# Attention in pairs of units: another order of one core's products, with norm weights and value pads made on chip

## The chip, the core and the metric

The kernel runs on one core of a Trainium2 chip. The core has five engines, each with an instruction queue of its own: TensorE (PE, with its weight loads listed as PEld), VectorE (DVE), ScalarE (ACT), GpSimd (POOL) and SyncE (SP, which here issues nearly all DMAs). They meet through semaphores. The metric is the device time of one execution in microseconds.

## What is computed

Three stages: attention with a bias that a small network computes from positions, a gated layer behind an RMS norm, and a layer with a squared ReLU.

```python
def _attn_ref(q, k, v, w1, b1, w2):          # q, k, v: 2 x 8 x 576 x 64
    scores = scale * np.matmul(q, k.transpose(0, 1, 3, 2))
    x = (psi_rel / psi_i)[..., None]         # log1p of distance / log1p of row
    h = np.maximum(x @ w1 + b1, 0.0)         # 32 hidden values per pair of positions
    bias = h @ w2                            # 8 heads
    scores = scores + bias.transpose(2, 0, 1)[None, :, :, :]
    scores = scores - np.max(scores, axis=-1, keepdims=True)
    attn = np.exp(scores)
    attn = attn / (np.sum(attn, axis=-1, keepdims=True) + 1e-09)
    return np.matmul(attn, v)
def _moe_ref(x, w_gate, w_val, w_out, rms_g):    # 1152 x 512, 1536 wide
    xn = x / np.sqrt(np.mean(x * x, axis=-1, keepdims=True) + 1e-06) * rms_g
    g = xn @ w_gate
    return (g * (1.0 / (1.0 + np.exp(-g))) * (xn @ w_val)) @ w_out
def _moe2_ref(x, w_in, w_out, s, b):             # 2048 wide
    r = np.maximum(x @ w_in, 0.0)
    return (s * (r * r) + b) @ w_out
```

## The kernel before

**Units.** Attention works on nine token tiles of 128 rows (eight of one batch each, the ninth with 64 rows of both). A tile is four units, each a pair of heads, so there are 36 units, `u` from 0 to 35. What is done for a unit:

- *scores* (`scores_mm`, L235): 64x64 products of q and k for both heads into the two buffers of `psA`, two PSUM banks each.
- *soft* (L248), once for each head `e`: one DVE operation adds the bias row and takes the row minimum of the negated sum. *expo* (L260): ACT's exponential with the row sum.
- *turn* (`turn_mm`, `turn_out`, L266 to L282): nine 128x128 transposes into `psB`, four for each head (`e0`, `e1`) and one for the rest of both (the tail). ACT evacuates e0 and the tail; DVE evacuates e1, but for every fourth unit from 6 to 29, where ACT does.
- *values* (`values_mm`, L284): products with v on 128x32 tiles into the one bank of `psO`.

**Bias rows.** 36 groups `g` of 16 rows. `hide(g)` (L176) computes the hidden values `hq`, four operations of 304 to 576 columns; from group 12 on POOL does one of them and DVE three. `bias_mm` (L189) is one visit of PE on 128x32 tiles, into one bank of `psB` or two where there are more than 512 columns; `bias_out` (L205) is two or three ACT operations. Groups 0 to 7 go to the bias buffer at once, the others are stored to DRAM (`rows`) and come back skewed by `bias_in` (L215). `bias` has two buffers, one for each chunk of two tiles.

**Finishing a tile.** `finish_a`: ACT copies `psO` out. `finish_t`: four PE transposes. `finish_b`: DVE divides by the row sums. `finish_s`: DVE sums squares, POOL raises to the power -1/2 (`rstd`). `finish_n` (L341): DVE scales by `rstd` and the norm weights `g_bc`. `finish_c`: four transposes, ACT's cast (L350) and DVE's subtraction (L351) give the high and the low part of `xs`, the operand of the next stage.

**Order.** The schedule is manual: each engine executes in the order in which the program writes its instructions. The loop at L473 runs step `s` once per unit: bias products of one group (`groups(s)`), scores of unit s+1, transposes of s, values of s-1, with one finishing function per step and `hide(s+13)`. `psB` has three banks in turn, `pr` (the exponentials) and `pt` (the transposed ones) two buffers each. `PT_DVE`, `SUMS`, `TAIL` and `BITS` (L452 to L455) tell at which steps operations of the next stage are issued: weights are fetched, clamped, put together from the bits of 64-bit numbers and split, and POOL makes sums of `xs`. After the loop the products of the next stage begin (`prod`, L624).

**Loads.** k and v tiles are loaded one per step on SP; a v tile is 128 x 10 x 64 with two half slots of zeros that come from DRAM with it. `g_bc` is loaded with a DMA that repeats one row on 128 partitions.

## Time and profile before

| | us |
|---|---|
| median of three runs (lowest, highest) | 599.57 (599.15, 600.49) |
| the profiled execution | 599.94 |
| its span, first to last instruction | 598.1 |
| PE busy in the span | 591.7 |
| DVE busy | 437.0 |
| ACT busy | 337.8 |
| POOL busy | 233.5 |

Busy time says who works, not who is waited for: the end of a matmul is modelled, so a PE that is 99% busy may still be at less than its peak. What a stage is bound by is read from its own window, and there from the steps between the starts of PE's groups: an interval that repeats to a hundredth of a us and has no releaser beside it is PE's own; one that varies, with a wait in brackets, is somebody else's. An idle engine costs nothing unless it is waited for.

### The profile page before, as it was taken

The page shows a single profiled execution, that of the slowest core. Times are in us where ns is not written, and L with a number is a line of the kernel's source. Part 1 is how long each engine was busy: PE and PEld are TensorE (multiplying, and loading weights), DVE is VectorE, ACT ScalarE, POOL GpSimd, SP SyncE. Part 2 cuts the span into 40 slices and gives each one's busy share as a digit, 9 for nine tenths or more (in the row PEclk, how much of TensorE's full clock was granted, in tenths as well). Part 3 has the DMA queues.
Part 4 walks back from the last instruction along what each step waited for, and adds up shares of the span by engine and source line. Part 5 has one row for each costly group of instructions (what it writes and reads, how often), then busy time and mean ns, then how long its engine had stood idle before and what let it go on. Part 6 is the DMA issues. An engine that isn't in the chain of part 4 may idle for free.

```text
span 598.1 us, 13403 instructions
## 1 busy us (share of the span) xinstructions
PE 591.7 (99%) x5370; PEld 529.1 (88%) x5370; DVE 437.0 (73%) x791; ACT 337.8 (56%) x689; POOL 233.5 (39%) x209
## 2 busy tenths in 40 slices
PE   9999999999999999999999999999999999999997
PEld 5466666667779999999999999999999999999996
DVE  7977888976876887788788944568778445888741
ACT  7887887887765555555657432255554235555210
POOL 0424334622446655655644432322224233222430
PEclk9999999999999999999999999999999999999999
DMA  6899445465112232133222323212222322222421
GB/s 213 265 321 258 151 148 146 149 205 155 37 39 71 71 110 103 71 102 110 72 75 102 103 74 105 105 38 73 86 83 101 118 71 70 71 72 70 162 86 53
DMA packets 25885, 67.52 MB, mean 113 GB/s; under 512 B 3136, under 2 KB 4704, under 8 KB 25824
## 3 DMA queue, kind: packets, MB, share of 16 engines
q1 hardware_dynamic: 25776, 66.66, 34.6%
q8 instruction: 42, 0.69, 0.5%
q14 instruction: 19, 0.16, 0.1%
q10 hardware_dynamic: 48, 0.02, 0.0%
HBM read 53.47 MB, written 10.83 MB: 108 GB/s over the span
## 4 chain that ended last, share of the span: by engine, by line
PE 74%; DVE 15%; ACT 5%; issue 4%; POOL 2%; DMA 1%; DVEq 0%; ACTq 0%; SPq 0%; POOLq 0%
PE c L624 11%; PE b L624 7%; PE po L302 7%; PE a L244 6%; PE b L272 6%; PE c L601 5%; DVE f L857 5%; PE c L599 5%; PE c L600 5%; DVE hv L853 4%; PE b L189 3%; PE b L601 3%; PE b L600 3%; PE b L599 3%; ACT f L856 3%
## 5 line engine op out<-in xcount | busy, mean ns | idle before, releaser
L408 POOL TENSOR_TENSOR wlo<-wa,whi 128x512 fp32r<-128x512 f32 (+1 forms) x71 | 92.7, 1308 | 89.5 <-ACT whi L405 89.5
L382 POOL TENSOR_SCALAR wa<-wa 128x512 f32<-128x512 f32 x68 | 45.7, 672 | 118.0 <-ACT wa L381 111.2
L256 DVE CUSTOM_DVE_ANT_0 sn<-a,bias 128x576 f32<-128x576 f32 x72 | 51.7, 754 | 19.3 <-PE a L244 11.8
L381 ACT ACTIVATE wa<-wraw 128x512 f32<-128x512 f32 x68 | 45.7, 673 | 27.1 <-DMA wraw<-in_wo 23.7
L263 ACT ACTIVATE pr<-sn,nm 128x576 f32<-128x576 f32 x72 | 56.3, 782 | 1.5 <-DVE nm L256 1.5
L176 POOL TENSOR_SCALAR hq<-tab,c_sb,thr 128x384 f32<-128x384 f32 (+17 forms) x24 | 45.7, 1911 | 28.8 <-DMA bias<-br 20.5
L857 DVE SCALAR_TENSOR_TENSOR f<-hv,b_sb,f 128x384 fp32r<-128x384 f32 x48 | 39.6, 824 | 21.9 <-ACT f L856 21.9
L856 ACT ACTIVATE f<-hv,b_sb 128x384 fp32r<-128x384 f32 x48 | 29.6, 617 | 45.4 <-DVE hv L853 45.3
L405 ACT CAST whi<-wa 128x512 fp32r<-128x512 f32 x68 | 41.9, 617 | 19.8 <-DVE wa L393 19.5
L601 PE MATMUL c<-f,wlo 128*128 128x384 f32 (+1 forms) x150 | 49.9, 333 | 0.7 <-POOL wlo L408 0.7
L600 PE MATMUL c<-f,whi 128*128 128x384 f32 (+1 forms) x150 | 49.7, 331 | 0.0
L599 PE MATMUL c<-f,whi 128*128 128x384 f32 (+1 forms) x150 | 49.7, 331 | 0.0
L390 DVE TENSOR_SCALAR wa<-wa 128x512 int32<-128x512 int32 x46 | 28.8, 625 | 25.4 <-POOL wa L382 25.4
L302 PE MATMUL po<-pt,vs 128*32 128x128 f32 (+1 forms) x1600 | 46.8, 264 | 0.0
L624 PE MATMUL c<-xs,whi 128*128 128x384 f32 x184 | 46.8, 335 | 0.0
L244 PE MATMUL a<-ks,q 64*64 64x352 f32 (+1 forms) x576 | 44.5, 415 | 0.2 <-ACT br L205 0.2
L281 ACT COPY pt<-b 128x512 f32<-128x512 f32 (+1 forms) x78 | 33.2, 435 | 20.4 <-PE b L272 20.1
L302 PEld LDWEIGHTS po<-pt,vs 128*32 128x32 f32 x1600 | 37.7, 110 | 5.8 <-issue 5.7
L244 PEld LDWEIGHTS a<-ks,q 64*64 64x64 f32 x576 | 18.9, 132 | 26.8 <-issue 6.3
L272 PEld LDWEIGHTS b<-ident,pr 128*128 128x128 f32 x288 | 30.8, 140 | 12.2 <-issue 9.6
L176 DVE TENSOR_SCALAR hq<-tab,c_sb,thr 128x448 f32<-128x448 f32 (+17 forms) x87 | 40.3, 524 | 0.0
L272 PE MATMUL b<-ident,pr 128*128 128x128 f32 x288 | 39.6, 280 | 0.3 <-ACT pr L263 0.3
(188 smaller groups left out, 1624.7 us busy)
## 6 DMA issues: line engine op xcount, KB each, us to landing
wraw<-in_wo SPq DMA_DIRECT2D x28, 512.0 KB, 3.5
bias<-rows SPq DMA_DIRECT2D x32, 288.0 KB, 4.3
rows<-br SPq DMA_DIRECT2D x28, 295.5 KB, 3.1
wraw<-in_win SPq DMA_DIRECT2D x16, 512.0 KB, 3.5
wraw<-in_wg SPq DMA_DIRECT2D x12, 512.0 KB, 3.6
wraw<-in_wv SPq DMA_DIRECT2D x12, 512.0 KB, 3.7
vs<-in_v SPq DMA_DIRECT2D x8, 320.0 KB, 6.4
ks<-in_k SPq DMA_DIRECT2D x8, 288.0 KB, 5.8
```

What stands on the lines that cost most here:

```text
L176: eng.tensor_scalar(hq, src, w1_sb, thr[:, n:n + 1], op0=ALU.mult, op1=ALU.max)
L244: nc.tensor.matmul(ps[e][qc, f], qt[u // 4][ed, hp, qc], ks[b[i % len(b)] * NP + hp][ed, f], start=True, stop=True, tile_position=(e * D, ...
L256: nc.vector.tensor_tensor_reduce(out=sn, in0=ps, in1=bias[chunk(u)][:, h, :], scale=-1.0 / SCALE, scalar=3.0e38, op0=ALU.add, op1=ALU.min, ...
L263: nc.scalar.activation(prs[u][:, e * S:(e + 1) * S], sn, AF.Exp, bias=nm, scale=-1.0, accum_out=sums[u // 4][:, h:h + 1])
L272: nc.tensor.transpose(pT[:, c * P:(c + 1) * P], pr[:, o:o + P], ident)
L302: nc.tensor.matmul(dst, w, a, start=c == 0, stop=c == NQC - 1, tile_position=(0, o))
L408: nc.gpsimd.tensor_tensor(out=lo[:, c:c + step], in0=w[:, c:c + step].bitcast(F32), in1=hi[:, c:c + step].bitcast(F32), op=ALU.subtract)
L599: nc.tensor.matmul(ps, hi[:, ws], ah, start=first, stop=False)
L600: nc.tensor.matmul(ps, hi[:, ws], al, start=False, stop=False)
L601: nc.tensor.matmul(ps, lo[:, ws], ah, start=False, stop=last)
L624: nc.tensor.matmul(ps, w[i][:, (c0 + c) * P:(c0 + c + 1) * P], a[h][c], start=first and c == 0 and i == 0 and h == 0, stop=c == 1 and i == ...
L857: nc.vector.scalar_tensor_tensor(out=hl[:, cols(j)], in0=g2, scalar=b_sb, in1=hh[:, cols(j)].bitcast(F32), op0=ALU.add, op1=ALU.subtract)
```

## The change

The loop takes two units at a time: a step of an even `s` issues scores of s+1 with soft and expo, values of s-2 and s-1, the bias products and `hide` of two groups, scores of s+2 with soft, and then all eighteen transposes of s and s+1 (`turns`), with the exponentials of s+2 put in between. The tails of two units share a bank and one copy. `finish_t` and `finish_c` are issued within the transposes, the rest of finishing around them. `pr` gets a third buffer. The loads of k and v are listed by step (`LOADS`), and all rows that have been stored are loaded at the start of a step. The tables of the next stage's operations get even steps.

The norm weights come as one row with 128 ones behind it (`g_row`); a product of the ones with the row puts it on all partitions, and ACT copies it to `g_bc` before the first pair. The v tiles come without zeros, in two halves of 64 partitions whose slots are shifted against each other, and DVE writes the zeros.

```diff
-    pr_p = ring(att, "pr", 2, "right")
+    pr_p = ring(att, "pr", 3, "right")
     pt_p = ring(att, "pt", 2, "right")
+    tail_p = ring(att, "ptl", 1, "right")
...
+    g_row = tab_p.tile([1, DM + P], F32, name="g_row")
...
+    nc.sync.dma_start(out=g_row, in_=rms_g)
...
-    vs = [None] * (B * NP)
+    vs = [ac.tile([P, 10, D], F32, name=f"vs{n}") for n in range(B * NP)]
+    for t in vs:
+        for h in range(2):
+            nc.vector.memset(t[D - h * D:P - h * D, 9 * h], 0.0)
...
     def load_v(n):
-        t = ac.tile([P, 10, D], F32, name=f"vs{n}")
-        nc.sync.dma_start(out=t, in_=v[:, n])
-        vs[n] = t
+        for h in range(2):
+            ps = slice(h * D, h * D + D)
+            nc.sync.dma_start(out=vs[n][ps, h:h + 9], in_=v[ps, n])
...
-    load_v(0)
-    nc.sync.dma_start(out=g_bc, in_=rms_g.partition_broadcast(P))
...
-    def turn_mm(u, e):
-        pr = prs[u]
-        pT = psB.tile([P, 512], F32, name="b")
-        if e < 2:
+    def turns(s, mid):
+        us = [u for u in (s, s + 1) if u < NU]
+
+        def turn(u, e):
+            pT = psB.tile([P, 512], F32, name="b")
             for c in range(4):
                 o = e * S + e * D + c * P
-                nc.tensor.transpose(pT[:, c * P:(c + 1) * P], pr[:, o:o + P], ident)
-        else:
-            nc.tensor.transpose(pT[:, :P], pr[:, 512:640], ident)
-        return pT
-
-    def turn_out(u, e, pT):
-        w = 512 if e < 2 else P
-        t = pt_p.tile([P, w], F32, name=f"pt{e}")
-        on_act = e not in PT_DVE or 6 <= u < 30 and u % 4 == 2
-        (nc.scalar.copy if on_act else nc.vector.tensor_copy)(t, pT[:, :w])
-        pts[u, e] = t
+                nc.tensor.transpose(pT[:, c * P:(c + 1) * P], prs[u][:, o:o + P], ident)
+            t = pt_p.tile([P, 512], F32, name=f"pt{e}")
+            on_act = e not in PT_DVE or 6 <= u < 30 and u % 4 == 2
+            (nc.scalar.copy if on_act else nc.vector.tensor_copy)(t, pT)
+            pts[u, e] = t
+
+        order = [(u, e) for e in range(2) for u in us]
+        for i, (u, e) in enumerate(order):
+            if i == 3:
+                mid["e0"]()
+                mid.pop("fin", bool)()
+            turn(u, e)
+        mid.pop("fin", bool)()
+        if us:
+            pT = psB.tile([P, 512], F32, name="b")
+            for i, u in enumerate(us):
+                nc.tensor.transpose(pT[:, i * P:(i + 1) * P], prs[u][:, 512:640], ident)
+            t = tail_p.tile([P, 2 * P], F32, name="pt2")
+            nc.scalar.copy(t, pT[:, :2 * P])
+            for i, u in enumerate(us):
+                pts[u, 2] = t[:, i * P:(i + 1) * P]
+        mid["e1"]()
...
-                    w, a = (vt[:, 4 * e + c, d:d + 32], pm[e][:, c * P + c0:c * P + c0 + cols]) if c < 4 else \
-                        (vt[:, 8 + e, d:d + 32], tl[:, c0:c0 + cols])
+                    w, a = (vt[:, 1 + 4 * e + c, d:d + 32], pm[e][:, c * P + c0:c * P + c0 + cols]) if c < 4 else \
+                        (vt[:, 9 * e, d:d + 32], tl[:, c0:c0 + cols])
...
-    SUMS = [(26, s_full, (0, 0, 0)), (27, s_full, (3, 0, 2)), (28, s_full, (1, 1, 0)), (29, s_full, (2, 1, 2)),
-            (31, s_comb, (2, 1, 2, ALU.add)), (36, s_comb, (1, 0, 1, ALU.subtract))]
+    SUMS = [(26, s_full, (0, 0, 0)), (26, s_full, (3, 0, 2)), (28, s_full, (1, 1, 0)), (30, s_full, (2, 1, 2)),
+            (30, s_comb, (2, 1, 2, ALU.add)), (34, s_comb, (1, 0, 1, ALU.subtract))]
...
-    TAIL = [(22, w_fetch, 0), (22, w_fetch, 1), (27, w_clamp, 0), (28, w_clamp, 1), (31, w_split, 0), (31, w_fetch, 2),
-            (33, w_clamp, 2), (34, w_split, 1), (34, w_fetch, 3)]
-    BITS = {30: 0, 33: 1}
+    TAIL = [(22, w_fetch, 0), (22, w_fetch, 1), (26, w_clamp, 0), (30, w_clamp, 1), (32, w_split, 0), (32, w_fetch, 2),
+            (34, w_clamp, 2), (34, w_split, 1), (34, w_fetch, 3)]
+    BITS = {28: 0, 32: 1}
...
+    pg = psO.tile([P, 512], F32, name="po", tag="po")
+    nc.tensor.matmul(pg, g_row[:, DM:], g_row[:, :DM], start=True, stop=True)
...
-    for s in range(-2, NU + 1):
-        r = s % 4
-        if s >= 5 and r == 1:
-            finish_a(s // 4 - 1)
...
+    def steps(s):
+        return [x for x in (s, s + 1) if s > -1] or [s]
+
+    LOADS = {0: ((load_k, 3), (load_v, 0), (load_k, 4), (load_v, 1)),
+             2: ((load_k, 5), (load_v, 2), (load_v, 3), (load_k, 6)),
+             4: ((load_k, 7), (load_v, 4), (load_v, 5)), 6: ((load_v, 6), (load_v, 7))}
+
+    for s in [-2, -1] + list(range(0, NU + 2, 2)):
+        both = steps(s)
+        new = [u for u in ((s + 1,) if s < 0 else (s + 1, s + 2)) if 0 <= u < NU]
+        for x in both:
+            if x >= 0 and x % 4 == 0:
+                load_q(x // 4 + 1)
+            if x == -1:
+                load_k(2)
+        for fn, n in LOADS.get(s, ()):
+            fn(n)
+        if s == 6:
+            xs = [act_p.tile([P, NKC, NT], F32R, name=f"xs{i}", tag=f"x{i}") for i in range(2)]
+        landed = list(rows)
+        if s >= 0:
+            for g in landed:
+                bias_in(g)
...
+        if s == -1:
+            for g in landed:
+                bias_in(g)
+            ps = scores_mm(0)
+            groups(s)
+            keep_clock(3)
+            soft(0, 0, ps[0])
+            expo(0, 0)
+            soft(0, 1, ps[1])
+            expo(0, 1)
+            nc.scalar.copy(g_bc, pg)
+            hide(12)
+            continue
+        if s + 1 < NU:
+            ps = scores_mm(s + 1)
+            for e in range(2):
+                soft(s + 1, e, ps[e])
+                expo(s + 1, e)
         if s in BITS:
...
+        if s % 4 == 0:
+            next(part, None)
+        if s >= 6 and s % 4 == 2:
+            finish_n(s // 4 - 1)
+        for u in (s - 2, s - 1):
+            if u >= 0:
+                values_mm(u)
+        if s >= 4 and s % 4 == 0 and s <= NU - 4:
+            finish_a(s // 4 - 1)
+        for x in both:
+            groups(x)
+        for x in both:
+            hide(x + 13)
+        if s + 2 < NU:
+            ps = scores_mm(s + 2)
+            for e in range(2):
+                soft(s + 2, e, ps[e])
+        mid = {"e0": lambda: s + 2 < NU and expo(s + 2, 0), "e1": lambda: s + 2 < NU and expo(s + 2, 1)}
+        if s >= 4 and s % 4 == 0 and s <= NU - 4:
+            mid["fin"] = lambda: finish_t(s // 4 - 1)
+        if s >= 6 and s % 4 == 2:
+            mid["fin"] = lambda: finish_c(s // 4 - 1)
+        if s % 8 == 4:
+            for g in list(rows)[:1]:
+                bias_in(g)
+        turns(s, mid)
+        if s >= 4 and s % 4 == 0 and s <= NU - 4:
+            finish_b(s // 4 - 1)
+            finish_s(s // 4 - 1)
         next(part, None)
...
+        for x in both:
+            for at, fn, n in TAIL:
+                if at == x:
+                    fn(n)
+            for at, fn, arg in SUMS:
+                if at == x:
+                    fn(*arg) if fn is s_full else fn(arg)
...
-    va = np.zeros((P, B * NP, 10, D), np.float32)
-    va[:, :, 0:4] = vv[:, 0, :512].reshape(B * NP, 4, P, D).transpose(2, 0, 1, 3)
...
                                keep, w2blk, minv, mrow], axis=1),
```

## Rows read from the trace of the kernel before

**Rows 1.** Windows: length, busy us (count) by engine, PEclk, DMA, GB/s.

```profile
98.16:116.97 18.81, 18.81 (x312) 11.88 (x308) 16.64 (x39) 14.94 (x36) 9.88 (x5) 1.00 0.49 144
116.97:135.09 18.12, 18.12 (x329) 12.25 (x317) 13.69 (x33) 14.84 (x38) 3.48 (x2) 1.00 0.61 183
139.16:154.31 15.15, 15.15 (x270) 10.88 (x269) 10.78 (x26) 12.08 (x31) 7.48 (x7) 1.00 0.36 95
```

**Rows 2.** Timeline of PE without bias rows: start us, us, line, op, tiles.

```profile
142.66 1.20 PE L244 MATMUL a<-ks,q 64*64 64x352 f32 x16
143.79 1.09 PE L272 MATMUL b<-ident,pr 128*128 128x128 f32 x8
144.72 0.27 PE L274 MATMUL b<-ident,pr 128*128 128x128 f32 x1
144.92 1.30 PE L302 MATMUL po<-pt,vs 128*32 128x128 f32 x40
146.15 1.20 PE L244 MATMUL a<-ks,q 64*64 64x352 f32 x16
...
149.64 0.66 PE L347 MATMUL b<-ident,x 128*128 128x128 f32 x4
150.23 1.20 PE L244 MATMUL a<-ks,q 64*64 64x352 f32 x16
```

**Rows 3.** Timeline of PE while bias rows are computed.

```profile
83.28 0.66 PE L315 MATMUL b<-ident,oT 128*128 128x128 f32 x4
83.86 0.91 PE L189 MATMUL b<-hq,c_sb 128*32 128x416 f32 x8
...
91.18 1.30 PE L302 MATMUL po<-pt,vs 128*32 128x128 f32 x40
92.30 0.93 PE L189 MATMUL b<-hq,c_sb 128*32 128x448 f32 x8
93.16 1.20 PE L244 MATMUL a<-ks,q 64*64 64x352 f32 x16
```

**Rows 4.** Timeline of PE's weight loads (PEld), one unit.

```profile
90.05 0.86 PEld L272 LDWEIGHTS b<-ident,pr 128*128 128x128 f32 x8 [0.33 <-issue]
...
92.19 0.24 PEld L189 LDWEIGHTS b<-hq,c_sb 128*32 128x32 f32 x8
```

**Rows 5.** Timeline of DVE; in brackets the idle time before, and its releaser.

```profile
106.50 1.46 DVE L176 TENSOR_SCALAR hq<-tab,c_sb,thr 128x512 f32<-128x512 f32 x3
...
110.81 0.74 DVE L341 SCALAR_TENSOR_TENSOR x<-x,rstd,g_bc 128x512 f32<-128x512 f32 x1
111.47 2.15 DVE L176 TENSOR_SCALAR hq<-tab,c_sb,thr 128x528 f32<-128x528 f32 x3
...
135.81 0.69 DVE L351 TENSOR_TENSOR xs<-b,xs 128x512 fp32r<-128x512 f32 x1 [1.41 <-ACT xs L350]
...
144.00 0.76 DVE L256 CUSTOM_DVE_ANT_0 sn<-a,bias 128x576 f32<-128x576 f32 x1 [1.44 <-PE a L244]
```

**Rows 6.** Timeline of POOL in the bias stage.

```profile
107.45 9.09 POOL L176 TENSOR_SCALAR hq<-tab,c_sb,thr 128x512 f32<-128x512 f32 x4
```

**Rows 7.** Timeline of ACT and PE at the start of attention.

```profile
25.46 1.10 ACT L205 ACTIVATE br<-b,cb,c_sb 128x400 f32<-128x400 f32 x2
...
29.00 1.09 PE L272 MATMUL b<-ident,pr 128*128 128x128 f32 x8
...
29.70 0.59 ACT L281 COPY pt<-b 128x512 f32<-128x512 f32 x1
```

**Rows 8.** Timeline of the first us: DVE's first work, PE's first bias products.

```profile
2.82 0.30 DVE L155 TENSOR_SCALAR thr<-c_sb 128x144 f32<-128x144 f32 x1 [2.82 <-DMA c_sb<-in_cst]
...
6.02 11.80 PE L189 MATMUL a<-hq,c_sb 128*32 128x512 f32 x128
```

**Rows 9.** Timeline of PE: scores of unit 35, first product behind.

```profile
169.47 1.20 PE L244 MATMUL a<-ks,q 64*64 64x352 f32 x16
...
177.55 0.60 PE L624 MATMUL b<-xs,whi 128*128 128x384 f32 x2
```

More of the change, by code (lines that the diff above doesn't have):

```diff
@@ L410, in w_split @@
             wst[n] = hi, lo
-    NU = 4 * NTT
     NG = S // 16
@@ L508, in tile_kernel @@
-        if 0 <= s + 1 < NU:
-            expo(s + 1, 1)
-        next(part, None)
-        if s >= 6 and r == 2:
-            finish_s(s // 4 - 1)
-        if s >= 7 and r == 3:
-            finish_n(s // 4 - 1)
-        if s >= -1:
-            hide(s + 13)
+        if s % 4 == 0:
[7 more added lines that the diff above has]
+            finish_a(s // 4 - 1)
@@ L519, in tile_kernel @@
             nc.sync.dma_start(out=b_sb, in_=b_p)
-        if 0 <= s - 1 < NU:
-            values_mm(s - 1)
-        if s >= 5 and r == 1:
-            finish_t(s // 4 - 1)
-        if s == 6:
-            xs = [act_p.tile([P, NKC, NT], F32R, name=f"xs{i}", tag=f"x{i}") for i in range(2)]
-        if s >= 8 and r == 0:
-            finish_c(s // 4 - 2)
         if s == 26:
@@ L956, in _layout @@
         "cst2": np.concatenate([np.tile(f["w2"], (1, 16)), f["b1"].reshape(HID, 1)], axis=1),
-        "rms_g": f["moe_rms_g"],
+        "rms_g": np.concatenate([f["moe_rms_g"], np.ones(P, np.float32)])[None],
         "wg": tile_up(f["moe_w_gate"], 12), "wv": tile_up(f["moe_w_val"], 12),
```

46 lines of the change are left out of this document (10 added, 36 removed).

## The prediction

> **What bounds the kernel now.** I read the table of windows first. In the three windows of the attention stage PE is busy for the whole window at a granted clock of 1.00, while DVE has 16.64 of 18.81 us while bias rows are still computed, 13.69 of 18.12 where they end and 10.78 of 15.15 behind them; ACT lies at 14.94, 14.84 and 12.08, POOL lower [rows 1]. Since the end of a matmul is modelled, I checked a full PE against its timeline: every unit repeats at the same step and no line shows a wait. Without bias rows a unit is scores 1.13 us (142.66 to 143.79), nine transposes 1.13 (to 144.92), values 1.23 (to 146.15): 3.49 us [rows 2]. With bias rows it is longer by one group of bias products: 0.86 where 448 columns are computed [rows 3]. So PE's instruction stream sets the time of this stage, and an order that costs PE less is worth its full saving, as long as nobody becomes late. DVE is nearest to that: 88% in the first window [rows 1].
>
> The stage behind attention is products on PE from 177.55 on [rows 9]; I take an earlier end of attention to move all of it. The profiled execution took 599.94 us (span 598.1 and 1.84 around it), the median of the runs is 599.57. I sum against 599.94 and subtract 0.37 at the end.
>
> **The change, part by part.**
>
> *PE's order.* The PE instructions of a unit stay; their order goes from (bias, scores, transposes, values) per unit to (scores, values x2, bias x2, scores, transposes x18) per pair. What that is worth are the places where PE changes from one kind of tile to another. Values followed by bias products, the same 128x32 tile, take 1.12 (91.18 to 92.30) [rows 3]; followed by scores 1.23 [rows 2]: a change there costs 0.11. Eight transposes take 0.93 (143.79 to 144.72), so 0.116 each, and the ninth with its change 0.20: 0.084. Four transposes before scores take 0.59 [rows 2] against 4 x 0.116 = 0.465 inside a run: 0.125. Per pair I get
> - one change bias to scores, or values to scores, less: 0.11;
> - transposes 2 x 1.13 = 2.26 become 18 x 0.116 + 0.125 = 2.22: 0.04 less;
> - one visit of scores is now left towards values and not towards transposes. No row shows that. It costs at most the same 1.13 and at least 0.11 less, as if there were no change. What is exposed first is a weight load: eight of 128 columns take 0.86, eight of 32 columns 0.24 [rows 4], 0.107 and 0.03 each. I take the difference, 0.08 less.
>
> Together 0.23 per pair (0.15 to 0.26); 16 pairs stand between scores of unit 4 and scores of unit 35: **-3.7 us** (-2.4 to -4.2).
>
> *Finishing.* The two times four transposes of a token tile move into the run of transposes. While bias rows are computed one costs 0.58 (83.28 to 83.86) [rows 3] and the values ahead 0.11 more, 0.69; without bias rows 0.59 [rows 2]. Inside a run it is 0.465. Nine of the 15 in the loop stand in the bias stage, six behind it: 9 x 0.225 + 6 x 0.125 = **-2.8 us**.
>
> *New waits.* This is the other side. A run of transposes now fills five banks of the three of psB in a row, so each waits for the evacuation three before it. An evacuation by ACT starts 0.70 after its first transpose (29.00 to 29.70) and takes 0.59 [rows 7], the third bank behind it begins 3 x 0.465 = 1.40 later: just in time on ACT. In the eight pairs with finish_a, e1 of the first unit is copied by DVE behind two soft, some 0.1 late: 0.8 us in all. In the pairs with finish_c the DVE subtraction L351 waits for ACT's cast, which now stands behind an exponential. DVE stood still 1.41 us for that cast before [rows 5]; now e1's copy and the next soft are queued behind it, and scores wait for soft to free psA.
>
> How late it gets depends on the hidden rows. Both units' hq now stand in one block between soft of the first and soft of the second unit. Pair 18, from the start of its first scores: e1's copy, finish_b and finish_s of the pair before, three operations of 512 columns like finish_n (0.66, 110.81 to 111.47) and 0.4 of small ones, hold DVE to 2.2; two soft, about 0.7 each, to 3.6; finish_n to 4.2; six hq, which take 1.46 per three alone but 2.15 while POOL works too [rows 5], and POOL has its own four for 9.09 us [rows 6]: 4.0, to 8.2. The second scores start at 4.95 (1.05, 2 x 1.12, some 1.65 for two bias groups), and soft could start 1.34 behind (142.66 to 144.00) [rows 2, 5], at 6.3. It is through with psA at 9.6, PE with its transposes at 4.95 + 1.13 + 2.22 + 0.47 = 8.8. So 0.8 us is bare. The same working with smaller hq gives 0.05, 0.2 and 0.4 in pairs 6, 10 and 14. Pair 22 has two groups of two banks each in psB, 0.4; pairs 26 and 30 have no hq, 0.15 each. Sum 0.8 + 2.15: **+3.0 us** (1 to 7).
>
> *Queues passed.* On SP, bias_in now stands behind the loads of a pair and ahead of the next two stores of rows; the first one into a buffer of bias that is used again waits for soft of the buffer's last unit. What is queued behind it is due a pair later: 0. On POOL, rstd waits for ss at the end of a pair, with hq behind it that are due a pair later too: 0. If a pair of lead were not enough, soft would wait for rows, and PE with it.
>
> *SBUF ports.* The Trainium skill, page SBUF — State Buffer, section Who interferes with whom, says that a DVE instruction in a two-port mode and a GpSimd instruction exclude each other for a whole instruction. By that rule an hq of DVE could wait a whole POOL hq, 9.09 / 4 = 2.27 us, twice in a pair. In seven pairs with long hq that would be up to 4.5 us each against the 1.4 that the rows give, some 20 us more. This trace does not agree: three hq of DVE took 0.69 longer beside POOL [rows 5], not 2.27. The sum goes by the row; the rule's direction is the third rival's.
>
> *Start.* In the first pair ACT has between the exponentials of unit 1 and the fourth bank of transposes the copy of g_bc (like a copy of 0.59), two groups of bias_out at 1.10 and one evacuation of 0.59 [rows 7], 3.4 us; scores 1.13 and three banks 1.40 cover 2.5. The product for g_bc (512 columns, one row deep) is two PE instructions ahead of the first bias products. It costs nothing to 0.95, by a bias group of 448 columns at 0.86 [rows 3]; those products go at the pace of DVE's hq, 11.80 / 8 = 1.48 per group [rows 8], so I take 0.2. Beside this less is done by scores of unit 4: **+0.9 us** (0 to 2). The 16 memsets of 64 columns stand where DVE is idle for 2.82 us, waiting for c_sb; its operation on 144 columns takes 0.30 [rows 8], so they take at most 4.8 and at the least nothing; I take them as covered, and 2.0 bare is the other end. The repeated load of g_bc and the zeros of v go away, and 16 smaller v loads and a small g_row come in on SP; nobody waits for them: 0. In the first pair one q, two k, two v and three groups of rows are queued at once; each is due a pair later.
>
> *End.* From scores of unit 35 to the first product there are 8.08 us now (169.47 to 177.55) [rows 9]. After: scores 1.05, four values 4 x 1.23, transposes 2.22 and finish_c 0.47, 8.66, and some 0.45 of wait for the last copies, which no scores cover any more: 9.1. Of that 0.16 is work that stood ahead of unit 35 before (a unit of values at 1.25 against one of transposes). **+0.85 us** (0.3 to 1.5). The sums, fetches and clamps of the next stage shift by a unit at most; the fetch of raw weights 3 waits for the last bit operation on weights 1, which now ends nearer to the end of attention, but it is clamped two products on: 0, and up to 1 if it is late.
>
> **Sum**: -3.7 - 2.8 + 3.0 + 0.9 + 0.85 = -1.75: 598.2 profiled, **597.8 us** as a median.
>
> **Rivals.**
> *The order works without waits.* The new waits come to nothing, since DVE's copies catch up and hq meet POOL less often; for it speaks that ACT's evacuations fit to a tenth. 597.8 - 3.0 = 594.8.
> *The gain is eaten.* Scores to values cost a full change (+1.3): 599.1, no difference. PE executes the same instructions, so the change may do little more than regroup; the new waits have the size of the gain.
> *DVE becomes the bound.* In the pairs 10 to 22 all hq fall beside POOL's. Against 1.46 that is 0.69 more per three, 1.4 per pair; half of it was in my reckoning. As soon as DVE's block ends later than PE's run of transposes, every further us stands on PE, since scores wait for psA. Seven pairs at 0.6 more: +4.2, **602.0**. For it speaks 88% of DVE [rows 1], against it that windows 10 us later have 76%.
>
> **How the numbers follow.** A measurement of this kernel can tell about 0.2%, 1.2 us, from no change. Forecast (partial gain) 0.40, without waits 0.22, eaten 0.20, DVE bound 0.18. Faster by more: 0.22, and 0.33 of the forecast's 0.40: 0.55. Within: 0.07 + 0.20 = 0.27. Slower: 0.18. The range goes from the waitless case with a little more saved at the changes of tile (594.2) to just below the DVE case (601.4).
>
> **What would show it.** Right: scores to values about 1.05, eighteen transposes and four of finishing in one run of 2.7 us, attention's first L624 some 1.8 us earlier, waits of PE at L244 for DVE in pairs 14 to 22 and at transposes for a copy of pt. Wrong: if PE shows no such waits (first rival), if scores stay at 1.13 (second), or if L244 waits over a us in each pair with hq (third). The prediction falls as well if the products behind attention do not move with it.

## The result, and the profile after

The changed kernel takes **607.23 us** (median of six runs, 606.06 to 609.8) against 600.75 for the kernel before on the same chip: ratio 1.0119 [1.0091, 1.0148]. It is slower by 1.2%, where 597.8 us was predicted, and lies outside the predicted range.

The profiled execution is the longest of the six, 609.8 us, span 608.0, 9.9 more than the span before; it holds 2.6 us more than the median. Both traces can be laid side by side by the starts of scores in PE's timeline. The windows below go from scores(4) to (12), to (22), to (28), to (35), and to the first product of the next stage; columns as in [rows 1]. Before:

```profile
36.07:70.76 34.69, 34.62 (x600) 22.89 (x596) 28.39 (x76) 28.62 (x69) 10.53 (x8) 1.00 0.84 248
70.76:116.97 46.21, 46.21 (x762) 29.33 (x758) 40.68 (x95) 37.69 (x90) 26.53 (x15) 1.00 0.50 150
116.97:142.66 25.69, 25.69 (x463) 17.69 (x451) 19.37 (x48) 19.88 (x50) 3.49 (x3) 1.00 0.65 191
142.66:169.47 26.81, 26.81 (x515) 19.37 (x511) 20.95 (x49) 20.90 (x54) 12.55 (x10) 1.00 0.16 44
169.47:177.55 8.08, 7.82 (x279) 6.42 (x279) 6.08 (x14) 4.19 (x11) 4.16 (x4) 1.00 0.19 69
```

After:

```profile
39.23:76.62 37.39, 34.48 (x600) 23.71 (x596) 29.36 (x73) 27.75 (x64) 13.83 (x10) 1.00 0.81 221
76.62:124.10 47.48, 46.46 (x763) 30.51 (x759) 44.14 (x97) 37.38 (x88) 22.71 (x14) 1.00 0.52 157
124.10:149.72 25.62, 25.11 (x462) 17.60 (x450) 19.09 (x46) 19.37 (x46) 5.47 (x4) 1.00 0.65 193
149.72:177.13 27.41, 27.35 (x444) 20.19 (x440) 23.20 (x50) 20.36 (x48) 11.46 (x8) 1.00 0.19 53
177.13:186.96 9.83, 9.15 (x360) 7.54 (x359) 8.30 (x18) 5.98 (x14) 2.79 (x3) 1.00 0.02 5
```

The 9.9 us are: scores(0) at 20.46 instead of 17.76, +2.70; to scores(4) +0.46; then +2.70, +1.27, -0.07, +0.60; the end +1.75; behind it +0.4. Attention was to become 1.75 us shorter; of its stretches only one did, by 0.07. Note DVE from scores(12) to (22): 44.14 of 47.48 us, 40.68 of 46.21 before, with two instructions more.

What answers to [rows 2], a pair without bias rows in PE's timeline after (start us, us, line, op, tiles):

```profile
146.27 1.20 PE L249 MATMUL a<-ks,q 64*64 64x352 f32 x16
147.40 2.39 PE L319 MATMUL po<-pt,vs 128*32 128x128 f32 x80
149.72 1.61 PE L249 MATMUL a<-ks,q 64*64 64x352 f32 x16
151.27 1.53 PE L278 MATMUL b<-ident,pr 128*128 128x128 f32 x12
152.66 0.66 PE L364 MATMUL b<-ident,x 128*128 128x128 f32 x4
153.15 0.65 PE L278 MATMUL b<-ident,pr 128*128 128x128 f32 x4
153.64 0.43 PE L294 MATMUL b<-ident,pr 128*128 128x128 f32 x2
154.00 1.20 PE L249 MATMUL a<-ks,q 64*64 64x352 f32 x16
```

The order itself works as drawn: the run of transposes takes 2.73 us (151.27 to 154.00). But scores are left in 1.13 us whether values follow (146.27 to 147.40) or, as before, transposes (142.66 to 143.79). The second scores take 1.61 where 1.20 is their own time: inside these 16 instructions PE waits for a bank of psA (e14 takes this wait away). It does not show as idle time of PE in these lines, only as a longer group.

The end, answering [rows 9]; in brackets the idle time before and its releaser:

```profile
177.13 1.20 PE L249 MATMUL a<-ks,q 64*64 64x352 f32 x16
178.26 2.44 PE L319 MATMUL po<-pt,vs 128*32 128x64 f32 x160
180.63 0.66 PE L278 MATMUL b<-ident,pr 128*128 128x128 f32 x4
181.84 1.09 PE L278 MATMUL b<-ident,pr 128*128 128x128 f32 x8 [0.55 <-ACT pr L268]
...
184.35 2.68 PE L319 MATMUL po<-pt,vs 128*32 128x64 f32 x160
186.96 0.62 PE L667 MATMUL b<-xs,whi 128*128 128x384 f32 x2
```

### The profile page after: what moved, and what is told of

It is laid out like the page before. It is cut to its first block, busy times and chain, and to the rows that moved or that the text cites. A ratio compares the mean times of both kernels' runs of the same rounds, so it can differ in the third digit from the quotient of the medians.

```text
span 608.0 us, 13408 instructions
## 1 busy us (share of the span) xinstructions
PE 594.0 (98%) x5372; PEld 531.1 (87%) x5372; DVE 448.0 (74%) x807; ACT 336.4 (55%) x672; POOL 233.7 (38%) x209
## 4 chain that ended last, share of the span: by engine, by line
PE 64%; DVE 17%; ACT 8%; issue 5%; DMA 3%; POOL 2%; SPq 0%; DVEq 0%; POOLq 0%; ACTq 0%
PE c L667 11%; PE b L667 7%; PE a L249 5%; PE c L644 5%; DVE f L900 5%; PE c L643 5%; PE c L642 5%; PE po L319 4%; DVE hv L896 4%; PE b L278 3%; PE b L643 3%; PE b L644 3%; PE b L642 3%; ACT f L899 3%; DMA ks<-in_k 2%
## 5 line engine op out<-in xcount | busy, mean ns | idle before, releaser
L249 PE MATMUL a<-ks,q 64*64 64x352 f32 (+1 forms) x576 | 48.9, 416 | 4.6 <-DVE nm L261 3.0
L407 DVE TENSOR_SCALAR wa<-wa 128x512 int32<-128x512 int32 x46 | 32.5, 707 | 26.8 <-POOL wa L399 26.8
L249 PEld LDWEIGHTS a<-ks,q 64*64 64x64 f32 x576 | 20.9, 132 | 29.0 <-DVE nm L261 8.3
L180 DVE TENSOR_SCALAR hq<-tab,c_sb,thr 128x448 f32<-128x448 f32 (+17 forms) x87 | 43.8, 568 | 1.5 <-PE b L193 1.5
L319 PE MATMUL po<-pt,vs 128*32 128x128 f32 (+1 forms) x1600 | 43.6, 263 | 0.5 <-DMA vs<-in_v 0.5
L667 PE MATMUL b<-xs,whi 128*128 128x384 f32 x152 | 38.8, 335 | 0.0
```

Of the source, the lines that this page charges most:

```text
L180: eng.tensor_scalar(hq, src, w1_sb, thr[:, n:n + 1], op0=ALU.mult, op1=ALU.max)
L249: nc.tensor.matmul(ps[e][qc, f], qt[u // 4][ed, hp, qc], ks[b[i % len(b)] * NP + hp][ed, f], start=True, stop=True, tile_position=(e * D, ...
L319: nc.tensor.matmul(dst, w, a, start=c == 0, stop=c == NQC - 1, tile_position=(0, o))
L667: nc.tensor.matmul(ps, w[i][:, (c0 + c) * P:(c0 + c + 1) * P], a[h][c], start=first and c == 0 and i == 0 and h == 0, stop=c == 1 and i == ...
```

## Experiments: which part of the change costs what

Each ratio is against runs of the kernel before on the same chip, whose median lay between 600.75 and 601.86. Experiments e1 to e4 ran on one chip, e5 to e8 on a second, e9 to e11 on a third, e12 to e15 on a fourth, e16 on a fifth; across chips the ratios are the safer comparison. A window or a timeline is of one execution.

**e1: the changed kernel, norm weights by the repeated load again.**

```diff
-    nc.sync.dma_start(out=g_row, in_=rms_g)
...
+    nc.sync.dma_start(out=g_bc, in_=rms_g.partition_broadcast(P))
...
-    nc.tensor.matmul(pg, g_row[:, DM:], g_row[:, :DM], start=True, stop=True)
...
-            nc.scalar.copy(g_bc, pg)
```

> The changed kernel with the norm weights loaded as before, by the repeated DMA; the product for them, its row and ACT's copy are gone. Theory: the product ahead of the first bias products holds PE back (in the changed kernel scores of unit 0 start at 20.46 us, 2.70 later than before), so scores of unit 0 start again near 17.8 and the time falls by 2 to 3 us, to about 604.5. Rival: the start is late because the first DMAs come in another order or because of the 16 memsets; then scores of unit 0 stay near 20.4 and the time stays within 1 us of 607.2.

Measured 607.14, ratio 1.0104 [1.0086, 1.0121]. Scores(0) start at 17.51, the 2.95 us of the start are back, but the median hardly moves (0.1 us, 0.9 by the ratios). In the profiled run 2.8 us are left at scores(8) and 0.9 at scores(12): the gain is lost again between them.

**e2: the changed kernel, v loaded whole with its zeros, no memsets.**

```diff
-            nc.vector.memset(t[D - h * D:P - h * D, 9 * h], 0.0)
...
-        for h in range(2):
-            ps = slice(h * D, h * D + D)
-            nc.sync.dma_start(out=vs[n][ps, h:h + 9], in_=v[ps, n])
+        t = ac.tile([P, 10, D], F32, name=f"vs{n}")
+        nc.sync.dma_start(out=t, in_=v[:, n])
+        vs[n] = t
```

> The changed kernel with v loaded as before, whole tiles with zeros from DRAM in one DMA each, and without the memsets. Theory: sixteen half loads hold SP (four of them took 3.63 us of its time against 0.45 for one whole load before) and rows stored behind them are late, so PE's waits for k and v (1.08 and 0.47 us) and DVE's wait of 3.23 us for the last bias row ahead of unit 8 shrink; 1.5 to 3 us less, about 605. Rival: the waits come from loading a whole pair at once, with v in one piece or two; then they stay and the time changes by less than 1 us.

Measured 606.34, 1.0086 [1.0067, 1.0105]. That is 0.9 us less than the changed kernel by the medians and 2.0 by the ratios, so the total does not tell the theory from its rival. PE's wait for ks and DVE's for the row are gone; a wait for vs is left, 0.87 us at 35.27. With whole loads the pair order has a wait there in some profiled runs (0.30 to 0.47 us in e7, e9, e11 and e14, 2.51 in e13) and none in others (e3, e15); the kernel before has none.

**e3: both undone, the pair order alone.**

> Only the order in pairs: norm weights and v as before. Theory: of the 7 us about 4 go with these two, and the order itself still loses some 2 to 3 us, to waits of scores for psA behind DVE (5 us between units 9 and 34 in the changed kernel) and 1.75 at the end: about 603. Rival: the order in pairs pays once the start and the loads are as before: 598 to 600.

Measured 603.74, 1.0048 [1.0031, 1.0065]. The two smaller edits together cost 3.5 us by the medians, 4.3 by the ratios. On the chip of e1 to e3 the half loads with the memsets cost 3.4 us without the product (e1), and the product 2.6 without the half loads (e2). The two costs do not add up: each hides in part in the delay of the other. The pair order, which was to bring the gain, costs 2.5 us by itself.

**e4: the kernel before with the norm product.** The edit of e1, the other way round, with ACT's copy at step 0.

> The kernel before with nothing but the norm weights by a product, at the place it has in the changed kernel. Theory: scores of unit 0 start at about 20.4 instead of 17.8 and the time rises by 2 to 3 us, all of it ahead of unit 0. Rival: beside the old order there is slack for it, under 0.8 us.

Measured 602.78, 1.0024 [1.0005, 1.0042], ten runs from 600.49 to 604.98. One thing that varies between executions is seen at the head of PE's timeline. The changed kernel:

```profile
5.97 2.05 PE L476 MATMUL po<-g_row 1*128 1x512 f32 x2
7.95 8.16 PE L193 MATMUL a<-hq,c_sb 128*32 128x512 f32 x80
...
20.46 0.81 PE L249 MATMUL a<-ks,q 64*64 64x352 f32 x4
```

And e2, the same product in the same place:

```profile
5.23 1.10 PE L473 MATMUL po<-g_row 1*128 1x512 f32 x2
6.26 11.76 PE L190 MATMUL a<-hq,c_sb 128*32 128x512 f32 x128
17.95 0.51 PE L246 MATMUL a<-ks,q 64*64 64x352 f32 x2
```

The product takes 1.10 or 2.05 us, and where it takes 2.05 the bias products behind it are late too. The profiled run of e4 had 1.10, and its scores(0) at 17.83.

The difference is TensorE's clock. Each trace's record of the granted clock begins within the first 14 us, with 1.00, and products ahead of that point run at half the pace: in e2, where it begins at 4.36 us, the 128-column products of the head start 0.213 us apart before it and 0.112 behind it. It begins at 5.54 in e4 and 5.26 in e12, ahead of the product, which takes 1.10 in both. In the changed kernel it begins at 13.75: the product ran before it, sets of four bias products start 0.83 us apart until then and 0.42 to 0.44 right behind it. So PE was at the lower of its two levels (1.2 of 2.4 GHz) until 13.75 us; where the windows print 1.00 for that time, there is no record. In the 13 profiled runs without a product at the head the record begins between 4.87 and 7.42 us. That the product kept the clock low is not shown by this one execution.

**e5: as e4, with operands 128 rows deep.**

```diff
-    g_row = tab_p.tile([1, DM + P], F32, name="g_row")
-    nc.sync.dma_start(out=g_row, in_=rms_g)
+    g_row = tab_p.tile([P, DM + P], F32, name="g_row")
+    nc.vector.memset(g_row, 0.0)
+    nc.sync.dma_start(out=g_row[:1, :], in_=rms_g)
```

> The kernel before with the norm weights' product at the head, as in e4, but with operands of 128 rows instead of one (the other 127 rows are zeros, written by one DVE memset; nothing of the result changes). The one-row product alone gave 602.78 against 601.27, with single runs from 600.5 to 605. Theory A, the shallow operand is what delays the rise of TensorE's clock in part of the executions: here the runs draw together near the kernel before, 601.0 to 601.8, none above 603.5, scores(0) at 17.7 to 18.0. Theory B, it is the product's place ahead of the bias products (any product there shifts them): 602.5 to 603 again, with the same spread of some 4 us. The memset costs DVE about 0.5 us in time in which it waits for the constants anyway: 0 under both.

Measured 601.68, 0.9992 [0.9974, 1.0009], runs from 600.04 to 603.38. The median is where theory A wants it and the spread a little narrower, but the profiled run had the product at 1.84 us, with the clock's record beginning inside it, at 7.49, and scores(0) at 18.53. Its interval overlaps that of e4, and the unchanged kernel spread from 599.74 to 606.02 on the same chip, so it is not shown that the depth is the cause.

**e6: the changed kernel, the product behind the second set of bias groups.**

```diff
-    nc.tensor.matmul(pg, g_row[:, DM:], g_row[:, :DM], start=True, stop=True)
...
-            keep_clock(3)
+            nc.tensor.matmul(pg, g_row[:, DM:], g_row[:, :DM], start=True, stop=True)
```

> The changed kernel with the one-row product moved from the head of TensorE's queue to behind the second set of bias groups, where three filler products stand otherwise. Theory A, the product at the head is what costs the start 2.7 us (20.46 against 17.76): scores(0) at 17.4 to 18.0 and the total 604.5 to 605.5. Rival B, as in e1 (607.14, its start recovered but the gain lost by a wait of 3.8 us for a bias row at scores(9) and a fall of the clock behind it): scores(0) early again, the wait for the row at about 58 us there again, and a total of 606.5 to 607.5. What tells them apart beside the total: the stretch from scores(4) to scores(12), 37.4 us in the changed kernel, 34.7 before, about 39 under B.

Measured 608.07, 1.0101 [1.0078, 1.0125]: scores(0) at 17.67, scores(4) to (12) 37.81 us, DVE's wait at the row 3.20. Rival B, the total a little above its range. As long as v comes in halves, much of an earlier start is paid back before scores(12): of 2.8 us at scores(0) 1.5 are left there.

**Where that is paid.** In the changed kernel the fetch of the last bias row of a chunk is issued at 57.92, 6.9 us behind the stores ahead of it (SP's timeline), and DVE's soft step waits for it (the profile names b_sb, a transfer issued beside it, but soft reads the bias row, and in 17 of the 18 profiled runs, whatever the profile names, it starts 0.16 to 0.45 us behind the landing of this row):

```profile
51.01 1.80 SPq L213 DMA_DIRECT2D rows<-br  x2
57.92 0.54 SPq L227 DMA_DIRECT2D bias<-rows  x1
```

```profile
61.81 0.76 DVE L261 CUSTOM_DVE_ANT_0 sn<-a,bias 128x576 f32<-128x576 f32 x1 [3.23 <-DMA b_sb<-in_b_p]
```

What SP waits for ahead of the fetch is the landing of the row's own store (waits of SP from 20 to 75 us: total, times, longest):

```profile
SPq L227 <- DMA rows<-br: 9.0, 5, 4.8
```

The store issued at 51.01 lands at 57.90, 6.9 us later. This store takes 6.5 to 7.7 us in the four runs with half loads, and 5.1 to 5.7 in eight of the nine with the pair order and whole loads (6.7 in e10). The place is near its limit in the old order too: DVE stands 1.80 us there in the kernel before, and PE loses nothing; in the profiled run of e5, with the loads of the kernel before, it stands 3.16 and scores(9) lose 1.0.

In e1 DVE stands for 3.77 us there, scores(9) wait 1.54, and then the granted clock falls (windows of e1):

```profile
56.00:58.00 2.00, 2.00 (x21) 1.81 (x18) 0.00 (x0) 1.87 (x5) 1.98 (x2) 1.00 0.44 135
58.00:60.00 2.00, 0.83 (x7) 0.52 (x6) 0.45 (x1) 0.34 (x1) 0.00 (x0) 1.00 0.68 161
60.00:62.00 2.00, 1.63 (x12) 0.66 (x14) 1.27 (x5) 1.65 (x5) 0.00 (x0) 0.80 0.69 174
62.00:64.00 2.00, 2.00 (x26) 1.11 (x26) 2.00 (x5) 0.95 (x3) 0.00 (x0) 0.50 0.95 303
64.00:66.00 2.00, 2.00 (x68) 1.95 (x64) 1.48 (x5) 1.41 (x4) 0.00 (x0) 0.85 0.73 256
```

PE was busy 0.83 of 2 us between 58 and 60; then it runs at the lower of its two levels (1.2 of 2.4 GHz): 0.80, 0.50 and 0.85 in three windows of 2 us are 0.8, 2.0 and 0.6 us of it.

**e12: the changed kernel, rows ahead of the last v loads on SP's queue.**

```diff
-        for fn, n in LOADS.get(s, ()):
-            fn(n)
+        if s < 6:
+            for fn, n in LOADS.get(s, ()):
+                fn(n)
...
+        if s == 6:
+            for fn, n in LOADS[6]:
+                fn(n)
```

The two scalar constants follow these loads too.

> The changed kernel with one change of order on SyncE's queue: in the pair at s = 6 the bias rows that have landed are fetched first, and the four half loads of v (v6, v7) and the two scalar constants stand behind them instead of ahead. In the changed kernel the last row for scores(8) and (9) is issued at 57.92 us, and the soft step of scores(8) at 61.81 waits 3.23 us. Theory A, the row is late because of what is queued ahead of it on SyncE: it is issued some 3 us earlier, the wait falls under 1 us, scores(4) to scores(12) takes 34.5 to 35.5 us instead of 37.39, total 604.5 to 605.8 against 607.2. Rival B, the row is late because its own store lands late (4.8 us there) or because the DMA engines are full (0.81 of their time, 221 GB/s): the wait stays over 2 us and the total at 606.5 to 607.5.

Measured 610.66, 1.0147 [1.0109, 1.0184], above both ranges; DVE's wait is 3.62 us, its row is issued at 58.63, 7.25 behind the stores, and scores(7) wait 1.61 for ks. Rival B by the wait. But the edit could not free this row: in the changed kernel too, the last loads of v are issued behind it, at 59.60. What shows rival B is the trace: the row's own store is issued at 51.38 and lands at 58.62, and the fetch goes out 0.01 later.

**e16: the pair order alone, v in two issues by columns.**

```diff
-        nc.sync.dma_start(out=t, in_=v[:, n])
+        for c in (slice(0, 5), slice(5, 10)):
+            nc.sync.dma_start(out=t[:, c], in_=v[:, n, c])
```

> The pair order alone (e3, v loaded whole with its pads) with each of the eight loads of v cut in two issues by columns: 128 partitions and 160 KB each, in place of 64 partitions and 144 KB each in the changed kernel. Against e3, putting the halves and the memsets of the changed kernel in costs 3.4 us (e1, 607.14 against 603.74). Theory A, the cost is the number of issues: 16 in place of 8 on SyncE's queue, each held 0.4 to 0.9 us ahead of rows and k: this kernel is at 606 to 607.5, with a wait for a bias row over 2 us at scores(8) or (9). Theory B, it is the shape, 64 partitions of 2.3 KB, which take nearly the landing time of a whole load (medians 5.5 to 6.2 us for 144 KB, 6.9 for 320 KB): here each half lands sooner, the total is 603.2 to 604.8, and no bias row is waited for over 1 us.

Measured 605.19, 1.0065 [1.0045, 1.0085]: between the two, with a wait of DVE of 1.71 us at that place. From scores(4) to (12) e3 takes 34.27 us (e14, the same program up to pair 24, 34.51), this one 35.93, e1 39.28. The DMA rows from 20 to 70 us (count, KB each, median us to landing), of e3, of this one and of the changed kernel:

```profile
vs<-in_v SPq DMA_DIRECT2D x8, 320.0 KB, 6.9
```

```profile
vs<-in_v SPq DMA_DIRECT2D x16, 160.0 KB, 5.0
```

```profile
vs<-in_v SPq DMA_DIRECT2D x16, 144.0 KB, 5.5
```

About half the bytes land in 0.72 to 0.80 of the time (6.2 us, 0.90, for the half loads of e1). Over the same 50 us the queue had the engines busy for 90.0% of the time at 245 GB/s in the changed kernel and 86.6% at 236 in e1, with whole loads 85.7% at 261 in e3 and 87.2% at 262 in the kernel before. So both count: a third of the loss in this stretch (1.66 of 5.01, one execution each; 1.0 of 3.4 by the ratios of the whole) came with the number of issues alone, and the rest comes with the half-width shape and with the clock that falls behind the wait; the two runs do not separate these.

## Experiments: why the pair order brings no gain

**e7 and e8: hidden tiles of groups 12 to 35 left out, in the pair order and in the kernel before.**

```diff
     def hidden(g):
+        if g > 11:
+            hms[g] = kept[9 + g % 3]
+            return
...
+        kept[g] = hms[g]
+        d = S if g > 8 else reach(g)
```

> The pair order alone (e3), with the hidden values of the bias groups 12 to 35 left out: their products take the tiles of the groups 9 to 11 again, so those bias rows are not the reference's; all else is done, DVE and POOL lose some 96 instructions between 19 and 150 us. To be set beside e8, the kernel before with the same left out. Theory A, what eats the gain of the order is DVE's block in pairs with s % 4 = 2 (finish_n and six hidden tiles, 3.5 to 4.5 us) ahead of the soft step, and so TensorE's wait for a scores tile: from scores(4) to scores(35) this kernel is 2 to 4.5 us shorter than e8, and in total 0 to 3 us faster (its end stays 1.7 longer). Rival B, the order itself gains nothing on TensorE (the dearer exit from scores to values and the longer chains take it): the same stretch is within 1 us of e8's, and the total 2 to 3 us above e8, as e3 stands above the kernel before (603.74 against 601.27).

> The kernel before with the hidden values of the bias groups 12 to 35 left out in the same way (their bias rows are not the reference's). If DVE doesn't bound the kernel before, as the prediction had it, 0 to 1.5 us are gained: 599.8 to 601.3. If DVE's block is a limit there too: 596 to 599.

Measured e7 602.28, 1.001 [0.9994, 1.0025], and e8 600.75, 0.9992 [0.9974, 1.001]. Scores(12) to (22) is 44.46 us in e7, 46.21 in e8 and 47.48 in e3 (windows in this order):

```profile
71.74:116.20 44.46, 44.44 (x763) 30.00 (x759) 25.21 (x62) 36.76 (x88) 1.09 (x2) 1.00 0.53 157
70.88:117.09 46.21, 46.21 (x762) 29.32 (x758) 26.11 (x64) 37.62 (x90) 1.09 (x2) 1.00 0.51 151
70.59:118.07 47.48, 46.47 (x762) 30.52 (x759) 44.14 (x97) 37.37 (x88) 22.72 (x14) 1.00 0.49 149
```

Here the pair order has its gain, 0.35 per pair, and the hidden tiles take 3.0 us away; the kernel before does not notice them. But scores(4) to (35) is only 1.1 shorter than in e8, between the two theories, since the rest of the stage has waits of its own, and the end costs 1.9.

**e13: the pair order without GpSimd's tiles, DVE's kept.**

```diff
+            if tq == POOL_QUAD and g >= POOL_FROM:
+                h_p.at["hq"] += 1
+                hms[g].append(kept[0])
+                continue
...
```

> The pair order alone (e3) with GpSimd's hidden tiles left out (one of four of each bias group from 12 on; its products take one fixed tile, so a quarter of those rows' sum is not the reference's). DVE keeps all its tiles and their place. Theory A, GpSimd beside DVE stretches DVE's tiles (six took 4.13 us beside GpSimd and 2.85 where it stood still), and that is what makes DVE late: the six take 2.9 to 3.1 us, scores(12) to scores(22) takes 44.5 to 45.5 us (47.48 in e3, 44.46 in e7 without any of the tiles), total 602 to 602.8. Rival B, DVE's own tiles are too many for the place between the two soft steps, whatever GpSimd does: 46.5 to 47.5 us, total 603.2 to 604.

Measured 602.23, 1.0015 [1.0, 1.003]; scores(12) to (22) 44.49 us, theory A at the lower end of its numbers. The pair around scores(16) and (17), first in the changed kernel (POOL, DVE, PE):

```profile
92.97 5.97 POOL L180 TENSOR_SCALAR hq<-tab,c_sb,thr 128x448 f32<-128x448 f32 x3
...
94.27 4.13 DVE L180 TENSOR_SCALAR hq<-tab,c_sb,thr 128x448 f32<-128x448 f32 x6
98.31 0.75 DVE L261 CUSTOM_DVE_ANT_0 sn<-a,bias 128x576 f32<-128x576 f32 x1
...
99.12 1.86 PE L249 MATMUL a<-ks,q 64*64 64x352 f32 x16 [0.41 <-DVE nm L261]
```

and in e13:

```profile
90.17 2.65 DVE L188 TENSOR_SCALAR hq<-tab,c_sb,thr 128x448 f32<-128x448 f32 x6
...
94.54 1.20 PE L257 MATMUL a<-ks,q 64*64 64x352 f32 x16
```

The same six tiles take 4.13 us beside GpSimd and 2.65 without it, and PE's scores lose 0.41 + 0.66 us for it. So it is GpSimd beside DVE, and not the number of DVE's own tiles: leaving those out as well (e7) brings the stretch no further. A single tile of DVE takes at most 1.02 us in that stretch of e3 and 0.57 in e13. The Trainium skill, page SBUF — State Buffer, section Who interferes with whom, has a DVE instruction in a two-port mode and a GpSimd instruction exclude each other for the whole instruction. The direction agrees; a whole instruction of GpSimd is 1.99 us here, and no tile of DVE was held for that long. Whether DVE's tiles run in such a mode, no run shows.

**e15: every second of GpSimd's tiles on ScalarE.**

```diff
-ACT_EARLY = (0, 1, 2, 3, 4, 5, 6, 7, 10)
+ACT_EARLY = (0, 1, 2, 3, 4, 5, 6, 7, 10) + tuple(range(12, 36, 2))
...
+            eng = nc.gpsimd if tq == POOL_QUAD and g >= POOL_FROM and g not in ACT_EARLY else nc.vector
```

In these groups ScalarE takes one of DVE's tiles, and DVE takes GpSimd's.

> The pair order alone (e3) with every second of GpSimd's hidden tiles (the even groups from 12) made on ScalarE, as the early groups' are. What is computed stays. GpSimd has one tile a pair instead of two, ScalarE one of about 0.65 us more a pair (it is busy 37.4 us of 47.5 between scores(12) and scores(22)). Theory A, as for e13, GpSimd's presence stretches DVE: DVE's six take about 3.4 us, scores(12) to scores(22) takes 45 to 46.3 us, total 601.8 to 603. Rival B: 47 us or more there, since ScalarE's tile delays the copies of the transposes by what DVE gains: 603.5 to 605.

Measured 605.85, 1.0072 [1.0049, 1.0095]; scores(12) to (22) 47.68 us. Rival B, the total a little above its range: DVE falls to 42.15 us there, ScalarE rises to 40.16, and PE now waits for ScalarE's copies of transposes ahead of the finishing ones (3.1 us in eight places from 36 to 174 us, by the waits).

**e9: bias products and hidden tiles ahead of the values.**

```diff
+        for x in both[:1] if s > 19 else both:
+            groups(x)
+        for x in both[:1] if s > 19 else both:
+            hide(x + 13)
         for u in (s - 2, s - 1):
             if u >= 0:
                 values_mm(u)
...
-        for x in both:
+        for x in both[1:] if s > 19 else ():
             groups(x)
-        for x in both:
             hide(x + 13)
```

> The pair order alone (e3) with the bias products and the hidden tiles of a pair moved ahead of its value products (in the pairs from 20 on only those of the first unit, since the last groups take two banks each). Theory A, what costs the pair order its gain is the place of DVE's block: the six hidden tiles can't begin before the bias products give their buffers free, these stand behind 2.2 us of values, and so the block ends 3 to 4 us later, after the scores of s + 2 have long been there. Then the block ends before those scores here, the first scores of the pairs 8, 12, 16 and 20 take 1.13 to 1.2 us instead of 1.8, scores(12) to scores(22) takes 44.3 to 45.3 us (47.5 in e3, 44.5 in e7 without the tiles, 46.2 before), and the total is 600.5 to 602 against 603.74 of e3. Rival B, it is DVE's sum of work in those pairs, wherever it stands: 46.8 to 47.5 us and 603.2 to 604. Rival C, the bias products now stand behind ScalarE's exponentials for their banks: idle TensorE ahead of them, 604 or more.

Measured 605.68, 1.0062 [1.0045, 1.0079]; scores(12) to (22) 47.74 us. Theory A fails, and rival C is nearest: the wait moved to the banks, but DVE holds them and not ScalarE (waits of PE in e9):

```profile
PE b L189 <- DVE x L337: 2.8, 5, 0.6
PE b L189 <- DVE xs L364: 1.3, 5, 0.4
```

**e11: the pair order, subtraction behind the last copy, weight bits at a pair's end; e10: the same on e9.**

```diff
-        nc.vector.tensor_tensor(out=xs[1][:, :, cs], in0=src, in1=xs[0][:, :, cs].bitcast(F32), op=ALU.subtract)
+        return lambda: nc.vector.tensor_tensor(out=xs[1][:, :, cs], in0=src, in1=xs[0][:, :, cs].bitcast(F32),
...
-        if s % 4 == 0:
-            next(part, None)
...
+        if s % 4 == 2:
+            next(part, None)
```

> The pair order alone (e3) with only the two moves on DVE of e10, the bias products behind the values as in e3. If the two are separate causes: scores(28) to scores(35) as in e10 (26.0 to 26.8 us against 27.4), scores(12) to scores(22) within 0.8 of e3's 47.5, and a total of 602.5 to 603.3. If the late copy is what ends the pairs with hidden tiles too, scores(12) to scores(22) falls by over 1 us, and the total is near e10's.

> e9 with two more moves on DVE: the subtraction of the low half of x is issued behind the copies of the transposes instead of ahead of the last one (it waits there 0.7 to 2.3 us for ScalarE's cast), and the first piece of the next stage's weight bits stands at the end of a pair instead of ahead of its second soft step (1.83 us there at 151.14 in e3). If the waits of scores(28) to scores(35) are DVE's (27.4 us in e3, 27.4 in e7, 26.8 before), this stretch falls to 26.0 to 26.8, and the total to 599.5 to 601.3. If they are the length of the chain from scores over soft step and exponential to the transposes, the stretch stays at 27.4 and the total at that of e9.

Measured e11 604.81, 1.0053 [1.0038, 1.0068], and e10 606.35, 1.0084 [1.0066, 1.0103]. Scores(28) to (35) is 27.27 us in both, 27.40 in e3: neither step ends that stretch.

**e14: finishing of DVE behind the next soft steps, from pair 24 on.**

```diff
+            if s > 24:
+                finish_b(s // 4 - 1)
+                finish_s(s // 4 - 1)
...
-            finish_b(s // 4 - 1)
-            finish_s(s // 4 - 1)
+            if s < 24:
+                finish_b(s // 4 - 1)
+                finish_s(s // 4 - 1)
```

> The pair order alone (e3) with one move in the pairs from 24 on, where no hidden tiles are made: DVE's scaling and sum of squares of a finished tile (about 2 us, at a pair's end, ahead of the soft step of the next scores) are issued behind the two soft steps of those scores. Theory A, the scores at 28 and 32 wait (1.61 and 1.87 us instead of 1.20) because that finishing work delays the soft step that frees their bank: both take 1.20 here, scores(28) to scores(35) is 26.4 to 26.9 us instead of 27.40, and the total falls by 0.5 to 1.2 to 602.5 to 603.2. Rival B, the wait only moves, to the finishing transposes or to the second soft step: 27.2 to 28.2 us and 603.5 to 604.5.

Measured 605.5, 1.0071 [1.0048, 1.0093]. The scores at 28 and 32 take 1.20 us, so it was DVE's finishing that they waited for. The stretch is 27.31 us all the same, rival B, with the wait at the next place:

```profile
162.51 0.63 PE L360 MATMUL b<-ident,x 128*128 128x128 f32 x4 [0.22 <-DVE x L354]
...
164.37 0.44 PE L290 MATMUL b<-ident,pr 128*128 128x128 f32 x2 [0.80 <-DVE pt L277]
```

Its end took 10.32 us. The total lies above both ranges, but up to pair 24 this is the program of e3, and scores(12) start at 71.81 us here and at 70.59 there: a total that differs from e3's by a us or two is no measure of an edit that acts later, and the stretches behind scores(12) are. No experiment made the pair order faster than the kernel before; the nearest, e7 and e13, leave work out.

## Why the prediction was wrong

The pair order without the product was forecast at -1.95 us and came to +2.5 (e3); the norm product and the re-cut loads, forecast at 0.2, came to 3.5. By terms:

*PE's order and finishing, -6.5.* Mechanism right but for one term, size too large. Run of transposes 2.69 forecast, 2.73 measured; values two at a time as forecast. Scores towards values were taken at 1.05, from the rows of weight loads, and are 1.13: that term came to nothing, as the second rival priced it. Without waits a pair gained 0.34 with bias rows (1.72 over five pairs in e13) where 0.455 was forecast, and 0.26 without (7.31 against 2 x 3.49 + 0.59): over ten and six pairs some -5.0.

*New waits, +3.0.* The step that failed worst inside the pair order. The working for pair 18 had the right chain, DVE's six tiles beside GpSimd ahead of soft, but mis-sized it: the scores after pairs 10, 14 and 18 lost 0.66, 1.07 and 1.27 us where 0.2, 0.4 and 0.8 stood. The other terms: 0.45 at pair 22 (forecast 0.4); and 0.41, 0.08, 0.67 and 0.25 at scores(28) to (34), where 0.3 stood for two pairs. Together 4.9. That is the third rival's mechanism, at about half the extra price it was given: 1.6 of the 1.9 us over the forecast stand at the first three places.

*"Nobody waits for them: 0", and queues passed, 0.* This failed outright. The rows' stores and the fetches behind them share the DMA engines with v, and those were busy for 90.0% of the time from 20 to 70 us. The waits are 1.65 us at scores(9) (0.59 in e3) and 1.8 for ks and vs in the changed kernel; its stretch from scores(4) to (35) is 3.35 us longer than e3's (137.90 against 134.55). "Due a pair later" was read off the program's order, without the landing times of the stretch from 20 to 70 us, which no row shows. Adding the -5.0, 4.9 and 3.35 gives +3.25 from scores(4) to (35); 4.5 were measured. Of the other 1.2 the 0.59 at scores(9) of e3 is a part, and the rest are short waits that I did not follow.

*Start, +0.9.* The product was priced at 0.2 by DVE's pace; the profiled run lost 2.70 there, those of e2 and e4 0.1 to 0.2. The 2.70 came with the clock at its lower level until 13.75 us, for which the sum had no term. From the medians it costs 1.5 on the kernel before (e4). The memsets took 2.55 us in DVE's idle time: covered, as said.

*End, +0.85.* 1.75 measured, 1.74 in e3; beside the 9.1 us of the forecast stand 9.83. The four values took 4.98 us (4.92 forecast); from 180.63 to 184.35 the transposes took 3.72, that is 0.99 of wait where 0.45 was allowed, most of it for ScalarE's exponential of unit 35 (0.55).

The chances were set as if the only doubt lay in the pair order; the prediction names the case that soft waits for rows, but gives it neither a price nor a chance.

## What to carry to other kernels

Regrouping a full engine's work saves what its changes of tile cost, tenths of a us here, but it also makes the gaps between its steps unequal, and every other engine's block must now fit the short gap: look for the longest block of each engine beside whatever stretches it, not for its busy share. Price a re-cut load by the landing times of the stretch in which it runs, and follow the chain store, fetch, consumer, before writing 0 for it. When two edits each delay the same consumer, undoing one alone can show little of its cost; undo both.

## What was not expected of the hardware

A product of one operand row at the head took 1.10 us in some executions and 2.05 in others, with the bias products behind it slowed as well until about 14 us (21 and 24 of them in the windows from 8 to 12 us, 29 and 29 in e2), while the windows print a clock of 1.00 for both. The record of the granted clock tells them apart: it begins at 13.75 us in the changed kernel, at 4.36 in e2. Why the clock rose so late in that execution stayed open. In e1 a stretch in which PE was busy 0.83 of 2 us was followed by some 3.4 us at a granted clock of 0.50; with the waits around it scores(4) to (12) took 5.0 us more than in e3.
